# Half-product gate and value projections in three more token blocks of a fused attention and gated feed-forward kernel

## The chip, the cores and the metric

The kernel runs on one core of one Trainium2 chip. The metric is the device time of one execution in microseconds, as the median over several runs. A core has TensorE (PE: matmuls, with weight loads shown as PEld), VectorE (DVE), ScalarE (ACT), GpSimd (POOL) and SyncE (SP), each with its own queue in program order. PSUM, where TensorE writes, has eight banks here, each of 128 partitions by 512 numbers of 32 bits.

## The reference

Inputs are q, k and v of shape (batch 8, heads 8, sequence 576, head size 64), a norm weight of 64 numbers, and four weight matrices. Attention has no softmax; its normalised output is the input x of a gated feed-forward layer:

```
kv  = einsum("bhsd,bhse->bhde", k, v)
o   = einsum("bhsd,bhde->bhse", q, kv)
x   = (o / sqrt(mean(o*o, -1) + 1e-6) * g_norm)   -> 4608 tokens x 512
g   = x @ w_gate        (512 x 1536)
val = x @ w_val         (512 x 1536)
ffn = (gelu(g) * val) @ w_out      (1536 x 512)
out = x + sigmoid(x @ w_res) * ffn
```

## The kernel before

**Tiling.** The 4608 tokens are nine blocks of 512. Blocks 0 to 7 hold the first 512 tokens of each batch; block 8 holds the 64 tokens left over from each of the eight batches, two batches to a slice of 128. Matmul operands are float16, sums are float32 in PSUM.

**A block's stages.** (1) Gate and value: twelve column tiles of 128 columns of each matrix; gelu on ScalarE and the product with the value on VectorE give `hid`. (2) The residual gate: 16 matmuls (`rps`) and tanh. (3) The output phase: `hid @ w_out` and the gate, the sum with x and the store.

**Direct tiles and half products.** A column tile is done directly by `m_gval`: four matmuls of 512 columns for the gate, four for the value. Alternatively `gv_group` does four column tiles at once by splitting tokens, inner dimension and columns in halves and forming seven products in place of eight: 56 matmuls of 256 columns for both matrices, in place of 32 of 512. This needs sums of the weights (`weight_sums`, formed once per group of four tiles, tiles named ws) and sums of the tokens (`token_sums`, once per block, tile ts). `GROUPS` lists which of the three groups of a block go by products: groups 1 and 2 in blocks 2 to 5, all three in blocks 6, 7 and 8; block 1 does none, block 0 one. What is left over is done directly, first. The output phase uses the same scheme with its own sums (`out_by_products`).

**A group's words.** `gv_group` runs a list of words, each a step for gate (g) or value (v):

```
1g 1v Eg 5g Ev 5v dg 6g dv 6v Fg 2g Fv 2v 7g g11 7v cg 3g cv 3v h11 g22 4g g12 h12 4v g21 h22 h21
```

A word with a digit first is a product of four matmuls (L736). Products 1, 6, 7 and 4 go through PSUM bank A, 2 adds to E, 5 and 3 use F. E is a seed, A copied to bank E on ScalarE (L746); d keeps product 5 in SBUF on ScalarE (L750); F and c are VectorE sums of A and d (L757), F back to PSUM and c to SBUF; g is a gelu of a quarter on ScalarE (L767); h the product with the value, on VectorE, or on POOL for quarter 22 (L773). Product 6 overwrites A after E has read it, 7 after F has, 4 after c has. The next group begins in another A bank and swaps E and F.

**Other work is hung between.** The order on each queue is written out by hand. `at(block, slot, ...)` puts functions behind a slot: slots 0 to 11 are the column tiles (a group takes the slot of its first tile), 12 and on are the residual gate and output phase. `at_word(block, i, word, ...)` puts them behind a word of the block's i-th group, `aside_out(block, key, ...)` inside the output phase, whose keys in order are D, gates, F, 00, 22, 01, 11, end. pf (L531) is the gating of a quarter by VectorE, c22 the sum ahead of the last quarter; fin (L535) the sum with x on POOL.

**Attention runs two blocks ahead.** In block m, `plan_attn_ahead` computes batch b = m + 2: `by_token` (L129, two halves on ScalarE) reorders q; `d_qT` and `d_rem_qT` (L363, L371) are transposing DMAs on SP of q and of the 64 left-over rows; `load_behind` makes POOL wait for these (copies into `hold`, L1136 to L1140) and then issues the loads of batch b + 1; `a_rem_kv` forms k-v sums on TensorE and the left-over output (`rem_mm`, L272), `kv_out` and `rem_out` (L281, L291) copy them out; `a_o` (L230) is the output of the 512 tokens; `a_ss` squares on ScalarE (L249) and reduces on VectorE (L254); `a_norm` is the inverse root on POOL, twelve small steps (L306 to L319, result ny); `a_t` (L345) scales by it, `a_x` (L359) by the norm weight; `d_xT` (L376) transposes x by DMA. Part of `a_t`, `a_x` and `d_xT` falls into block m + 1. Until now batch 7 alone, whose scaling falls into block 6, has these at words of groups; batches 4 to 6 have them at slots of direct tiles.

**Buffers.** A tag names a ring of buffers; a new tile waits for the last reader of the one that held its place.

Of the kernel before, what the change touches and what calls it, by code (L numbers as in the profile page):

```python
# [8 lines left out]
FP32 = mybir.dt.float32  # L9
# [9 lines left out]
def kernel(  # L19
# [18 lines left out]
    C = H * D  # L38
# [89 lines left out]
    def by_token(b, copy=nc.vector.tensor_copy, js=slice(0, NJ)):  # L128
        copy(  # L129
            out=b16_t[b, "q"].rearrange("p j h d -> p h j d")[:, :, js, :],  # L130
            in_=raw[b, "q"].rearrange("p h (j d) -> p h j d", j=NJ)[:, :, js, :],
        )
# [35 lines left out]

    def attn_begin(b):
        st[b] = {  # L170
            "qT": attnp.tile([P, NJ, NP, P], FP16, tag="qT", name="qT"),
            "kv2": (
                attnp.tile([P, NP, D], FP16, tag="kv2", bufs=4, name="kv2")
                if b > 0
                else consts.tile([P, NP, P], FP16, name="kv0")
            ),
            "ss": attnp.tile([P, NJ + 1, H], FP32, tag="ss", name="ss"),
            "o": {},
        }
# [101 lines left out]
        nc.scalar.copy(out=st[b]["kv2"], in_=st[b]["ps"][0])  # L281

    def rem_out(b):
        if b < B - 1:
            o32 = attnp.tile([P, C], FP32, tag="o32", name="o32")
        else:
            o32 = qkvp.tile([P, H, NJ * D], FP16, tag="k16", name="o32")
            o32 = o32.rearrange("p a b -> p (a b)").bitcast(FP32)[:, 0:C]
        st[b]["o"][NJ] = o32
        for e in range(2):  # L290
            nc.scalar.copy(  # L291
                out=o32.rearrange("p (r e d) -> p r e d", e=2, d=D)[:, :, e, :], in_=st[b]["ps"][1][e]
            )
# [207 lines left out]
    def out_by_products(blk, later, banks, amid):  # L501
        w = {}
        s_ = hid_sums

        def aside(ahead_of):
            for f in amid.get(ahead_of, ()):
                f()

        def res(jj):
            for j in (2 * jj, 2 * jj + 1):  # L510
                m_res(blk, j, banks[j])

        def first_two():
            for n in ("D", "E", "F", "A"):
                w[n] = pmoe.tile([P, 2, CH], FP32, name="w" + n, bank=banks[n])
            w["d"] = attnp.tile([P, 2, CH], FP32, tag="o32", name="wd")
            s_last(blk)
            prod(w["A"], a_of(blk, 1, 1), b_of(1, 1), True)
            nc.scalar.copy(out=w["E"], in_=w["A"])
            aside("D")  # L520
            prod(w["D"], s_[0], wo_t[:, 0], True)
            nc.scalar.copy(out=w["d"], in_=w["D"])
            aside("gates")
            for j in range(NJ):
                m_sigmoid(j)

        def part(jj):
            return slice(None), slice(2 * jj[0], 2 * jj[0] + 2), slice(jj[1] * CH, (jj[1] + 1) * CH)

        def pf(jj, src):  # L530
            nc.vector.tensor_tensor(out=res_all[part(jj)], in0=th_all[part(jj)], in1=src, op=ALU.mult)  # L531

        def fin(jj):
            of = part(jj)
            nc.gpsimd.tensor_tensor(out=res_all[of], in0=res_all[of], in1=t_t[blk][of], op=ALU.add)  # L535

        def store(jj):
            dst = out[blk * S : blk * S + M0, :].rearrange("(p j) c -> p j c", j=NJ)
            js = slice(2 * jj, 2 * jj + 2)
            nc.sync.dma_start(out=dst[:, js, :], in_=res_all[:, js, :])  # L540

        def others():


            prod(w["A"], s_[1], wo_t[:, 1], False)
            aside("F")
            sub(nc.vector, w["F"], w["A"], w["d"], ALU.add)
            aside("00")
            prod(w["E"], a_of(blk, 1, 2), b_of(2, 1), False)
            pf((0, 0), w["E"])  # L550
            aside("22")
            prod(w["A"], s_[2], wo_t[:, 2], False)
            c22 = res_all[part((1, 1))]
            sub(nc.vector, c22, w["A"], w["d"], ALU.add)
            aside("01")
            prod(w["F"], s_[3], b_of(2, 2), False)
            pf((0, 1), w["F"])
            aside("11")
            prod(w["A"], a_of(blk, 2, 2), wo_t[:, 3], False)
            if len(GROUPS.get(blk + 1, ())) * GF < NF or blk + 1 >= LAST[0]:  # L560
                pf((1, 1), c22)
                pf((1, 0), w["A"])
            else:
                pf((1, 0), w["A"])
                pf((1, 1), c22)
            aside("end")
            if later:
                return
            for i in (1, 0):
                fin((i, i))  # L570
                fin((i, 1 - i))
                store(i)

        if later:
            x = [lambda j=j: a_x(blk, j) for j in range(NJ)]
            at_word(blk + 1, 0, "Fv", x[0])
            at_word(blk + 1, 0, "h21", *x[1:3], lambda: fin((0, 0)), lambda: fin((0, 1)), lambda: store(0))
            at_word(blk + 1, 1, "Fv", x[3], lambda: fin((1, 0)), lambda: fin((1, 1)), lambda: store(1))
        return [lambda: res(0), lambda: res(1), first_two, others]

    def out_last(blk, banks):
# [22 lines left out]
        def run():  # L604
            wa = [bank(1, banks["A"][e]) for e in range(2)]
            wd, we, wf = [bank(2, banks[n]) for n in "DEF"]
            d = attnp.tile([P, 2, CH], FP32, tag="o32", name="wd")
            u = attnp.tile([P, 2, CH], FP32, tag="sq", bufs=3, name="u")
            one = (slice(0, 1), slice(1, 2))
            s_last(blk)  # L610
# [96 lines left out]
    def gv_group(blk, g, banks, amid):  # L707
# [44 lines left out]
        def plus(u, n):  # L752
            if n == "F":
                dst = tile_of("F", u)
            else:
                dst = sb["c", u] = attnp.tile([P, 2, PR], FP32, tag="o32", name="c")
            nc.vector.tensor_tensor(out=dst, in0=ps["A", u], in1=sb["d", u], op=ALU.add)  # L757

        quarter = {"11": ("E", 0, 0), "12": ("F", 0, 1), "21": ("A", 1, 0), "22": ("c", 1, 1)}
# [383 lines left out]
    def at(blk, slot, *fs):  # L1143
        plans[blk].setdefault(slot, []).extend(fs)
# [19 lines left out]
            at(m, 10 + j // 2, lambda j=j: a_x(b, j))  # L1164
        at(m, 11, lambda: d_xT(b, 0, NJ))

    GROUPS = {blk: (1, 2) for blk in range(2, B - 2)} | {B - 2: (0, 1, 2), B - 1: (1, 0, 2), B: (0, 1, 2)}
    amid_gv = {}

    def at_word(blk, i, word, *fs):  # L1170
        amid_gv.setdefault((blk, i), {}).setdefault(word, []).extend(fs)

    def plan_attn_ahead(b):

# [6 lines left out]
            begin.append(lambda: d_rem_qT(b))  # L1181
        if m in GROUPS:
            for i in range(2):
                at(m, 2 + i, lambda i=i: by_token(b, act, slice(2 * i, 2 * i + 2)))
            at(m, 3, *begin)
            if b + 1 < B:
                at(m, 2 * GF, lambda: load_behind(b))
        else:
            at(m, 8, lambda: by_token(b, act, slice(0, 2)))
            at(m, 9, lambda: by_token(b, act, slice(2, 4)), *begin)  # L1190
            at(m, NF - 1, lambda: a_kv(b, act))
            at(m, NF, lambda: load_behind(b))
        if rem:
            own = 2 * pair(b) + 1 == b
            at_word(m, 1, "5v" if own else "3v", lambda: a_rem_kv(b))
            at_word(m, 1, "5v" if own else "g12", lambda: kv_out(b))
            at_word(m, 1, "h21", *[lambda: rem_mm(b)] * own, lambda: rem_out(b), lambda: a_sq(b, NJ))
        at(m, NF, lambda: a_o(b), *[lambda: a_red(b, NJ)] * rem, lambda: a_ss(b, 0), lambda: a_ss(b, 1))
        aside_out(m, "D", lambda: a_ss(b, 2), lambda: a_ss(b, 3))
        aside_out(m, "F", lambda: a_norm(b, 0, NJ + rem, pool))  # L1200
        first = [lambda: new_block(b), lambda: a_t(b, 0), lambda: a_t(b, 1)]
        if b == B - 1:
            aside_out(m, "11", *first)
        else:
            at(m, NF + 3, *first)
        if b == B - 1:
            t = [lambda j=j: a_t(b, j) for j in range(NJ + 1)]
            x = [lambda j=j: a_x(b, j) for j in range(NJ + 1)]
            for i, word, fs in (
                (0, "1v", t[2:3]),  # L1210
                (0, "Fv", t[3:4]),
                (0, "h21", t[4:5]),
                (1, "1v", x[0:2]),
                (1, "Fv", x[2:3]),
                (2, "1v", [x[3], lambda: d_xT(b, 0, NJ), x[4], lambda: d_xT(b, NJ, NJ + 1)]),
            ):
                at_word(m + 1, i, word, *fs)
            return
# [13 lines left out]
    at(0, 6, *sums["v", 2][0:2])  # L1232
    at_word(0, 0, "Fv", *sums["v", 2][2:4])
    late_sums = [f for u in (("g", 0), ("v", 0)) for f in sums[u]]
    for i, f in enumerate(late_sums):
        at_word(2 + i // 2, i % 2, "Fv", f)
    for blk in GROUPS:
        t = token_sums(blk, nc.vector)
        if blk == 2:
            at(blk - 1, NF + 3, *t)  # L1240
            continue
        whole = blk == B - 2 and len(GROUPS[blk]) * GF == NF
        for key, f in zip(("00", "22", "01", "end" if whole else "11"), t):
            aside_out(blk - 1, key, f)
    out_at = {}

# [153 lines left out]
```

## Time and profile before

| | us |
|---|---|
| median of 5 runs | 326.55 (326.1 to 326.95) |
| the profiled execution, its run | 326.95 |
| its span, first to last instruction | 325.1 |
| TensorE busy | 317.0 |
| VectorE busy | 260.4 |
| ScalarE busy | 194.6 |
| POOL busy | 135.5 |

Spans of blocks in that execution, from TensorE's first instruction of each:

| block | start | end of gate and value | end |
|---|---|---|---|
| 2 | 91.80 | 112.09 | 125.40 |
| 3 | 125.40 | 145.64 | 158.94 |
| 4 | 158.94 | 179.18 | 192.48 |
| 5 | 192.48 | 212.97 | 226.28 |
| 6 | 226.28 | 244.96 | 257.58 |
| 7 | 257.58 | 275.92 | 288.55 |

A row of the profile names line, engine, operation and tiles; lengths of matmuls include their passage through the array and so overlap. A group row gives busy time, mean length and the idle time in front of it with what ended that. In a row of stages the columns are bounds, length, busy time and count of PE, PEld, DVE, ACT and POOL, TensorE's granted clock, DMA share and GB/s.

### The profile page before, as it was taken

What the parts mean: (1) busy time and instruction counts of PE and PEld (TensorE: products, weight loads), DVE (VectorE), ACT (ScalarE), POOL (GpSimd) and SP (SyncE); (2) the same over time, 40 slices, a digit from 0 to 9 for tenths busy, and PEclk for the clock granted to TensorE, in tenths of its full rate; (3) what the DMA queues carried; (4) which work ended last, traced back from release to release, by engine and by line L of the source; (5) the groups of instructions that cost most, each with busy time, mean ns of one, the idle gap of its engine ahead of it and who ended that gap; (6) DMA issues with size and microseconds to landing.
All of it is one profiled execution on the core that took longest, in us unless ns stands there. A gap on an engine that the chain in (4) does not pass through costs nothing.

```text
span 325.1 us, 7256 instructions
## 1 busy us (share of the span) xinstructions
PE 317.0 (97%) x2864; PEld 230.0 (71%) x2864; DVE 260.4 (80%) x477; ACT 194.6 (60%) x355; POOL 135.5 (42%) x205
## 2 busy tenths in 40 slices
PE   8989999999999999999999999999999999999993
PEld 3644754444858776787678676868887888788782
DVE  5788879669698999888888888798987677667754
ACT  3673685465727781868267837584766467636660
POOL 2793251572711787037712773114711242043232
PEclk9999999999999999999999999999999999999999
DMA  7999999699995499559958894900331030002004
GB/s 251 325 204 203 195 206 173 162 186 125 157 136 105 150 133 163 156 92 129 100 176 116 102 127 151 145 0 3 129 59 26 0 131 1 2 19 112 3 0 129
DMA packets 76692, 38.87 MB, mean 120 GB/s; under 512 B 42098, under 2 KB 74354, under 8 KB 76658
## 3 DMA queue, kind: packets, MB, share of 16 engines
q0 software_dynamic: 38752, 17.17, 42.0%
q1 hardware_dynamic: 37328, 20.71, 25.3%
q10 hardware_dynamic: 578, 0.52, 0.5%
q8 instruction: 22, 0.36, 0.5%
q14 instruction: 12, 0.10, 0.1%
HBM read 38.80 MB, written 9.44 MB: 148 GB/s over the span
## 4 chain that ended last, share of the span: by engine, by line
PE 96%; DVE 3%; issue 0%; DVEq 0%
PE wA L492 11%; PE Av L736 10%; PE Ag L736 10%; PE rps L419 10%; PE gps L399 9%; PE vps L399 9%; PE Fg L736 5%; PE Fv L736 5%; PE fps L436 3%; PE wF L492 3%; PE wE L492 3%; PE wD L492 3%; PE w L492 2%; PE Ev L736 2%; PE Eg L736 2%; PE idle L901 2%
## 5 line engine op out<-in xcount | busy, mean ns | idle before, releaser
L773 POOL TENSOR_TENSOR hid<-ge,c 128x512 f16<-128x512 f16 x18 | 20.9, 1162 | 84.8 <-ACT ge L767 84.8
L387 ACT ACTIVATE ge<-gps 128x512 f16<-128x512 f32 x36 | 21.3, 597 | 42.3 <-PE gps L399 42.2
L535 POOL TENSOR_TENSOR osb<-osb,t 128x512 f32<-128x512 f32 x28 | 31.8, 1164 | 32.8 <-DVE osb L531 31.0
L492 PEld LDWEIGHTS <-hid_s 128*128 128x128 f16 x384 | 37.6, 98 | 4.3
L399 PE MATMUL gps<-xT,wg 128*128 128x512 f16 x136 | 34.9, 379 | 0.0
L399 PE MATMUL vps<-xT,wv 128*128 128x512 f16 x136 | 34.9, 379 | 0.0
L419 PE MATMUL rps<-wr,xT 128*128 128x512 f16 x144 | 33.4, 380 | 0.0
L388 DVE TENSOR_TENSOR hid<-ge,vps 128x512 f16<-128x512 f16 x36 | 24.5, 685 | 9.3 <-PE vps L399 8.7
L492 PEld LDWEIGHTS <-hid 128*128 128x128 f16 x288 | 28.2, 98 | 5.0
L736 PEld LDWEIGHTS <-wsv 128*128 128x128 f16 x288 | 28.1, 98 | 3.9 <-issue 0.3
L736 PEld LDWEIGHTS <-wsg 128*128 128x128 f16 x288 | 28.1, 98 | 3.4
L757 DVE TENSOR_TENSOR Fg<-Ag,d 128x512 f32<-128x512 f32 x18 | 12.6, 699 | 16.9 <-PE Ag L736 13.4
L428 ACT ACTIVATE th<-rps 128x512 f32<-128x512 f32 x36 | 21.1, 594 | 7.8 <-PE rps L419 7.8
L399 PEld LDWEIGHTS <-wv 128*128 128x128 f16 x136 | 13.3, 98 | 16.1
L254 DVE TENSOR_REDUCE ss<-sq 128x8 f32<-128x512 f32 x32 | 20.1, 679 | 4.4 <-ACT sq L249 4.4
L419 PEld LDWEIGHTS <-xT 128*128 128x128 f16 x144 | 13.5, 98 | 14.2
L399 PEld LDWEIGHTS <-wg 128*128 128x128 f16 x136 | 13.1, 98 | 14.7 <-issue 0.2
L736 PEld LDWEIGHTS <-wg 128*128 128x128 f16 x216 | 20.9, 98 | 3.6
L767 ACT ACTIVATE ge<-c 128x512 f16<-128x512 f32 x18 | 11.3, 630 | 19.8 <-DVE c L757 19.8
L736 PEld LDWEIGHTS <-wv 128*128 128x128 f16 x216 | 21.1, 98 | 2.5
L736 PE MATMUL Av<-ts,wsv 128*128 128x256 f16 x144 | 21.6, 272 | 0.0
L736 PE MATMUL Ag<-ts,wsg 128*128 128x256 f16 x144 | 21.6, 273 | 0.0
(187 smaller groups left out, 741.5 us busy)
## 6 DMA issues: line engine op xcount, KB each, us to landing
out_dram<-osb SPq DMA_DIRECT2D x14, 512.0 KB, 2.7
qraw<-in_q_dram POOLq DMA_DIRECT2D x7, 512.0 KB, 6.8
k<-in_k_dram POOLq DMA_DIRECT2D x7, 512.0 KB, 8.5
v<-in_v_dram POOLq DMA_DIRECT2D x7, 512.0 KB, 10.9
wg<-in_moe_w_gate_dram POOLq DMA_DIRECT2D x2, 512.0 KB, 8.2
wv<-in_moe_w_val_dram POOLq DMA_DIRECT2D x2, 512.0 KB, 8.6
wo<-in_moe_w_out_dram POOLq DMA_DIRECT2D x2, 512.0 KB, 14.0
out_dram<-osb SPq DMA_DIRECT2D x4, 256.0 KB, 4.5
```

Of the source, the lines that this page charges most:

```text
L254: nc.vector.tensor_reduce(out=out_, in_=sqs.pop((b, i)), op=ALU.add, axis=mybir.AxisListType.X)
L387: nc.scalar.activation(out=ge, in_=gps, func=AF.Gelu)
L388: nc.vector.tensor_tensor(out=hids[blk][:, f, :], in0=ge, in1=vps, op=ALU.mult)
L399: nc.tensor.matmul(ps[:, j0 * P : j1 * P], lhsT=w[:, cc, :], rhs=xT_t[blk][:, j0:j1, cc, :], start=(cc == 0 and j0 == 0), stop=(cc == NP - ...
L419: nc.tensor.matmul(rps, lhsT=xT_t[blk][:, j, cc, :], rhs=wr16[:, cc, :], start=(cc == 0), stop=(cc == NP - 1),)
L428: nc.scalar.activation(out=th, in_=rps, func=AF.Tanh, scale=0.5)
L492: nc.tensor.matmul(ps[:, e - es[0], :], lhsT=a[:, f, e * P : (e + 1) * P], rhs=b[:, f, :], start=(start and e == es[0] and f == 0), stop=( ...
L535: nc.gpsimd.tensor_tensor(out=res_all[of], in0=res_all[of], in1=t_t[blk][of], op=ALU.add)
L736: nc.tensor.matmul(out_[:, r, :], lhsT=lhsT, rhs=rhs, start=(first and r == 0 and c == 0), stop=(c == 1), skip_group_check=True,)
L757: nc.vector.tensor_tensor(out=dst, in0=ps["A", u], in1=sb["d", u], op=ALU.add)
L767: nc.scalar.activation(out=ge[q], in_=source(q, "g"), func=AF.Gelu)
L773: eng.tensor_tensor(out=dst, in0=ge[q], in1=source(q, "v"), op=ALU.mult)
```

## The change

Blocks 3, 4 and 5 get all three groups by half products (`WHOLE = 3`); block 2 stays as it was, and blocks 6 to 8 too. What stood at slots of direct tiles moves: the copies of q to word g11 of groups 0 and 1, with the begin of attention and its transposes behind the second; the k-v sums and the left-over rows to the last group; the scaling and transposes of batches 4 to 6 to the places that batch 7 had. The last token sum goes ahead of pf(1,1). The weight sums of group 0, which were spread over the groups of blocks 2 to 5, go to slots 2, 6 and 7 and the output phase of block 1. Buffers: one for qT in place of two, three for the tag o32 (c and the left-over output, now for batch 7 too), and wd in the ring of the squares.

```diff
-            "qT": attnp.tile([P, NJ, NP, P], FP16, tag="qT", name="qT"),
+            "qT": attnp.tile([P, NJ, NP, P], FP16, tag="qT", bufs=1, name="qT"),
@@ rem_out
-        if b < B - 1:
-            o32 = attnp.tile([P, C], FP32, tag="o32", name="o32")
-        else:
-            o32 = qkvp.tile([P, H, NJ * D], FP16, tag="k16", name="o32")
-            o32 = o32.rearrange("p a b -> p (a b)").bitcast(FP32)[:, 0:C]
+        o32 = attnp.tile([P, C], FP32, tag="o32", bufs=3, name="o32")
@@ out_by_products (and out_last alike)
-            w["d"] = attnp.tile([P, 2, CH], FP32, tag="o32", name="wd")
+            w["d"] = attnp.tile([P, 2, CH], FP32, tag="sq", bufs=3, name="wd")
@@ others
-            if len(GROUPS.get(blk + 1, ())) * GF < NF or blk + 1 >= LAST[0]:
+            if whole(blk + 1):
+                pf((1, 0), w["A"])
+                aside("end")
+                pf((1, 1), c22)
+            else:
                 pf((1, 1), c22)
                 pf((1, 0), w["A"])
-            else:
-                pf((1, 0), w["A"])
-                pf((1, 1), c22)
-            aside("end")
@@ gv_group, plus
-                dst = sb["c", u] = attnp.tile([P, 2, PR], FP32, tag="o32", name="c")
+                dst = sb["c", u] = attnp.tile([P, 2, PR], FP32, tag="o32", bufs=3, name="c")
@@
-    GROUPS = {blk: (1, 2) for blk in range(2, B - 2)} | {B - 2: (0, 1, 2), B - 1: (1, 0, 2), B: (0, 1, 2)}
+    WHOLE = 3
+    GROUPS = {blk: (1, 2) for blk in range(2, WHOLE)} | {blk: (0, 1, 2) for blk in range(WHOLE, B - 1)} | {B - 1: (1, 0, 2), B: (0, 1, 2)}
+    def whole(blk):
+        return WHOLE <= blk < B - 1
@@ plan_attn_ahead
             for i in range(2):
-                at(m, 2 + i, lambda i=i: by_token(b, act, slice(2 * i, 2 * i + 2)))
-            at(m, 3, *begin)
+                half = lambda i=i: by_token(b, act, slice(2 * i, 2 * i + 2))
+                if whole(m):
+                    at_word(m, i, "g11", half)
+                else:
+                    at(m, 2 + i, half)
+            if whole(m):
+                at_word(m, 1, "g11", *begin)
+            else:
+                at(m, 3, *begin)
...
+            last = len(GROUPS[m]) - 1
...
-            at_word(m, 1, "5v" if own else "3v", lambda: a_rem_kv(b))
-            at_word(m, 1, "5v" if own else "g12", lambda: kv_out(b))
-            at_word(m, 1, "h21", *[lambda: rem_mm(b)] * own, lambda: rem_out(b), lambda: a_sq(b, NJ))
+            at_word(m, last, "5v" if own else "3v", lambda: a_rem_kv(b))
+            at_word(m, last, "5v" if own else "g12", lambda: kv_out(b))
+            at_word(m, last, "h21", *[lambda: rem_mm(b)] * own, lambda: rem_out(b), lambda: a_sq(b, NJ))
...
-        if b == B - 1:
+        if whole(m + 1):
             aside_out(m, "11", *first)
         else:
             at(m, NF + 3, *first)
-        if b == B - 1:
+        if whole(m + 1):
             t = [lambda j=j: a_t(b, j) for j in range(NJ + 1)]
@@ weight and token sums
-    for i, f in enumerate(late_sums):
-        at_word(2 + i // 2, i % 2, "Fv", f)
+    for i, f in enumerate(late_sums[0:6]):
+        at(1, (2, 6, 7)[i // 2], f)
+    for key, f in zip(("00", "22"), late_sums[6:8]):
+        aside_out(1, key, f)
...
-        whole = blk == B - 2 and len(GROUPS[blk]) * GF == NF
-        for key, f in zip(("00", "22", "01", "end" if whole else "11"), t):
+        for key, f in zip(("00", "22", "01", "end" if whole(blk) else "11"), t):
             aside_out(blk - 1, key, f)
```

More of the change, by code (lines that the diff above doesn't have):

```diff
@@ L606, in run @@
             wd, we, wf = [bank(2, banks[n]) for n in "DEF"]
-            d = attnp.tile([P, 2, CH], FP32, tag="o32", name="wd")
+            d = attnp.tile([P, 2, CH], FP32, tag="sq", bufs=3, name="wd")
             u = attnp.tile([P, 2, CH], FP32, tag="sq", bufs=3, name="u")
```

## The prediction

> **What bounds the kernel now.** I read the shares of busy time and the chain that ended last first, then the busy time by stage, then TensorE's instructions in order of time, and last the engines around one stall. The page's busy shares and its chain by engine:
>
> ```profile
> PE 317.0 (97%) x2864; PEld 230.0 (71%) x2864; DVE 260.4 (80%) x477; ACT 194.6 (60%) x355; POOL 135.5 (42%) x205
> ...
> PE 96%; DVE 3%; issue 0%; DVEq 0%
> ```
>
> TensorE sets the end: 96% of the chain is its own work. A busy TensorE says little by itself, so the next question is whether instructions start back to back. TensorE in order of time, block 5 (start, length, operation); the fourth row opens group 1, the last one group 2:
>
> ```profile
> 192.48 1.03 PE L399 MATMUL gps<-xT,wg 128*128 128x512 f16 x4
> 193.34 1.03 PE L399 MATMUL vps<-xT,wv 128*128 128x512 f16 x4
> ...
> 199.39 0.60 PE L736 MATMUL Ag<-xT,wg 128*128 128x256 f16 x4
> ...
> 205.50 0.60 PE L736 MATMUL Ag<-xT,wg 128*128 128x256 f16 x4
> ```
>
> The lengths overlap, so starts count. Four direct columns of gate and value take 199.39 - 192.48 = 6.91 us (32 matmuls of 512 columns), the same four columns by half products 205.50 - 199.39 = 6.11 us (56 of 256 columns). No idle time stands in either. The exchange is worth **0.80 us** wherever it is fed.
>
> Busy time by stage (bounds, length, then PE, PEld, DVE, ACT, POOL with counts, clock, DMA): the gate and value stages of blocks 3, 4 and 5 as they are, then of blocks 6 and 7, which already do all three groups by products:
>
> ```profile
> 125.40:145.64 20.24, 20.24 (x203) 14.93 (x201) 17.91 (x34) 12.81 (x23) 7.25 (x7) 1.00 0.70 131
> 158.94:179.18 20.24, 20.24 (x203) 14.94 (x200) 17.92 (x34) 12.81 (x23) 7.26 (x7) 1.00 0.59 118
> 192.48:212.97 20.49, 20.49 (x202) 14.80 (x200) 17.02 (x33) 12.94 (x23) 6.43 (x6) 1.00 0.56 119
> 226.28:244.96 18.68, 18.68 (x171) 16.41 (x168) 17.59 (x33) 12.43 (x24) 7.38 (x7) 1.00 0.32 92
> 257.58:275.92 18.34, 18.34 (x170) 16.43 (x168) 13.28 (x22) 12.35 (x24) 7.31 (x7) 1.00 0.15 59
> ```
>
> Block 7 is three groups at 6.11 us with nothing lost. Block 6 is 0.34 us longer: it also carries the scaling of batch 7 on VectorE (17.59 us busy of 18.68). That is what blocks 3 to 5 are about to look like. Where block 6 loses it: VectorE in order of time, then TensorE's pieces of the chain at that place:
>
> ```profile
> 225.79 1.29 DVE L345 TENSOR_TENSOR t<-op,ny 128x512 f16<-128x512 f32 x2
> 227.00 0.68 DVE L531 TENSOR_TENSOR osb<-th,wA 128x512 f32<-128x512 f32 x1
> ...
> 228.53 0.69 DVE L345 TENSOR_TENSOR t<-op,ny 128x512 f16<-128x512 f32 x1
> 229.13 0.69 DVE L757 TENSOR_TENSOR Fg<-Ag,d 128x512 f32<-128x512 f32 x1
> 229.73 0.69 DVE L757 TENSOR_TENSOR Fv<-Av,d 128x512 f32<-128x512 f32 x1
> ```
>
> ```profile
> 229.94 0.53 PE Ag L736 x4
> 230.47 0.00 issue
> 230.47 0.60 PE Av L736 x4
> ```
>
> A product takes 0.44 us; these two took 0.53 and 0.60. Product 7 overwrites A, so it waits until VectorE's Fg and Fv have read A, and those stand behind a full VectorE queue left from the output phase. Two later products lose 0.04 each: 0.09 + 0.16 + 0.08 = 0.33 us.
>
> **The change, part by part.**
>
> Group 0 by products in blocks 3 to 5. TensorE: -0.80 us in each, **-2.40** in all, if fed. VectorE: two Fg/Fv and two c sums (about 0.69 each) and three hidden products (0.68) for four of 0.68: +2.1 us of durations a block; less the two weight sums that leave each block (four half operations of 0.285, 1.1 us). ScalarE +2.4 us (two seeds, two keeps at 0.6), POOL +1.16 us. The stage then has the VectorE work of block 6, in the same words and order, since batches 4, 5 and 6 now get the placement that batch 7 has. So I take block 6's stall, 0.34 us a block: **+1.02**. Bounds: 0 (block 7's row) and 0.8 (where the gain is eaten).
>
> One rule speaks against this. The Trainium skill, "VectorE: DVE Perf Modes", section "The DRAIN you can't avoid", says that a VectorE operation does not start before the pipe of the one ahead has emptied (it allows an earlier start elsewhere on the page). Read so, the lengths add up. The rows above show starts 0.60 us apart (228.53, 229.13, 229.73) against lengths of 0.69. By the rule, some 14 operations until VectorE has caught up would end 14 x 0.09 = 1.3 us later, and a block would lose 1.3 + 0.34 - 0.80 = 0.84 us instead of gaining: 329.1 us in all. The measured starts contain whatever drain there is; I go by them.
>
> Scaling of the first two parts (t) ahead of pf(1,0), not after the block. In blocks 2 to 4 this now stands in the output phase, as in block 5 above (225.79 before 227.00). A late norm holds everything queued behind on VectorE: pf(1,0), which frees bank A for ScalarE's seed of Ev, the keeps d behind that seed, and Fg. The norm chain on POOL ends 225.76 - 226.28 = -0.52 us against the end of block 5's output phase; for blocks 2, 3 and 4 the same row ends at 124.88, 158.42 and 191.96, each -0.52 against 125.40, 158.94 and 192.48. So the position is the same, with no slack and no wait: counted in the 0.34.
>
> Query copies (by_token) moved from the direct columns to word g11 of groups 0 and 1: 1.04 us on ScalarE each. In block 6 ScalarE idles 1.50 and 1.03 us just there, waiting for c. Cost 0; if c came early, up to 0.1 us.
>
> Transposing DMAs: d_qT and d_rem_qT on SP now follow the second copy. With block 6's times that copy ends 11.26 us into the block. Two issues of block 4 now, and the landing of all four of the second kind:
>
> ```profile
> 169.59 2.55 SPq L363 DMA_TRANSPOSE qT<-q x1
> 172.31 1.52 SPq L371 DMA_TRANSPOSE qrT<-qr x1
> ...
> DMA to landing us min/median/max: 2.6/3.4/4.4
> ```
>
> The second issue comes at 11.3 + 2.7 = 14.0 and lands at 17.4 (16.6 to 18.4). TensorE wants it after word 3v of the last group: group 2 starts at 238.85 in block 6, twelve words at 0.437 later is 17.8 us into the block. The slack is 0.4 us, with an end of -0.6 in blocks 3 and 4 (batch 7 uses it only at h21). Behind it stand that batch's 40 k-v matmuls and products 4. I take 0: the 4.4 was measured with an xT transpose right in front in the queue, which now comes after. That xT pair ends near 19 us on SP and lands by about 22; the token sums read it at 28. POOL's hold ahead of the next loads comes after the last group, some 19 us, behind both landings. Half 0 of the copy, 1.1 us earlier than before, needs q: loads land 6.2 to 6.8 us after issue there, 8 us and more ahead of the copy.
>
> Token sum 4 ahead of pf(1,1), and pf order as block 5 has it: no operation added, cost 0.
>
> Weight sums of group 0 in block 1: eight of about 0.5 us. Slots 2, 6 and 7 hold two each (1 us); VectorE idled 1.46, 0.98 and 1.04 us at those slots, and the two left go to gaps of 0.60 and 0.57 us. POOL runs the norm beside some: one such pair took 0.88 instead of 0.48 beside a POOL operation. Then slots 6 and 7 run 0.8 us over, within the two-slot turn (3.46 us) of the banks. Cost 0; without that cover 0.5.
>
> Buffers: one qT less (its reader a_o ended a block ago), wd in the squares' turn (its predecessor was reduced over 2 us earlier: reductions end at 183.9, wd is written at 186.31), a third o32. Cost 0 each; a wait would show on ScalarE's wd copy.
>
> **Sum.** Blocks 3 and 4 hold 20.24 - 6.91 - 2 x 6.11 = 1.11 us of k-v matmuls and their gaps: 18.68 + 1.11 = 19.79, -0.45 each. Block 5: 1.36 likewise, 20.04 against 20.49, -0.45. Together **-1.35**. The profiled execution took 326.95 (span 325.1 and 1.85 around it), so its like would take 325.6, span 323.75. It lies 0.40 above the median of the runs; on the median, 326.55 - 1.35 = **325.2 us**.
>
> **The rivals.** *No stalls at all:* the end-of-stage slack absorbs them and TensorE gets 2.40 plus 0.1 of today's: 324.05. For it: block 7; against it: block 6 with the same VectorE queue. *Late remainder transpose:* qrT lands at its worst in blocks 3 and 4 and the wait is 0.6 each: 325.2 + 1.2 = 326.4, no change to speak of. *Slower:* the norm. Moved ahead of pf(1,0), each us that POOL's chain is late stalls product 7 in group 0 one for one, in blocks 3, 4 and 5, where before only the scaling itself slipped. From 0.45 us a block the gain is gone, from 0.7 us it is a loss that counts; at 0.9 us: 326.55 + 3 x 0.45 = 327.9. For it: zero slack, and loads' descriptors on POOL ahead of the chain in blocks 2 to 4 (not in block 5); against it: the chain began when its sums were ready and ended at the same -0.52. *That the products don't pay* is excluded by 6.11 against 6.91.
>
> **How the numbers follow.** About 0.2%, 0.65 us, is what a measurement of this kernel can tell from no change. Likeliest case 0.62 (324.6 to 325.8), no stalls 0.13, late transpose 0.12, late norm 0.10, other mixtures 0.03. The first two are faster: 0.75, and a little of the third: 0.77; the rest of the third and mixtures within: 0.12; slower 0.11. The range runs from 324.0 to 326.4: it takes in the first three cases and leaves 0.13 outside.
>
> **What would show it.** Right: stages of blocks 3 to 5 near 19.8, 19.8 and 20.0 us, short waits only at product 7 of group 0, copies of q in ScalarE's idle time ahead of c, qrT landed before 3v. Wrong: stages near 19.4 (no stalls), TensorE waiting at kvp L272 for qrT, VectorE's t waiting for POOL's ny, or block 1 longer than now.

## The result, and the profile after

The changed kernel takes 325.41 us as a median (325.19 to 326.15, 23 runs) beside 326.41 us for the kernel before (44 runs): a ratio of 0.9969, 95% interval 0.9962 to 0.9976, so about 1.0 us or 0.3% faster. The forecast was 325.2 us, or -1.35.

The profiled execution spans 324.0 us against 325.1. The busy shares and the chain by engine, after:

```profile
PE 316.0 (98%) x2936; PEld 236.8 (73%) x2936; DVE 265.6 (82%) x486; ACT 200.8 (62%) x367; POOL 140.0 (43%) x208
...
PE 96%; DVE 3%; issue 0%; DVEq 0%
```

TensorE still sets the end. The gate and value stages of blocks 2 to 6, after (columns as before):

```profile
91.56:111.80 20.24, 20.24 (x203) 14.93 (x201) 18.65 (x36) 12.81 (x23) 6.44 (x6) 1.00 0.71 115
125.10:145.01 19.91, 19.91 (x226) 17.24 (x224) 18.82 (x34) 14.83 (x27) 8.37 (x8) 1.00 0.65 129
158.31:178.23 19.92, 19.92 (x226) 17.21 (x224) 18.83 (x34) 14.82 (x27) 8.38 (x8) 1.00 0.49 121
191.53:211.71 20.18, 20.18 (x226) 17.15 (x224) 18.23 (x33) 15.16 (x27) 7.78 (x7) 1.00 0.51 113
225.02:243.83 18.81, 18.81 (x171) 16.41 (x168) 17.72 (x33) 12.43 (x24) 7.28 (x7) 1.00 0.36 84
```

Against 20.29, 20.24, 20.24, 20.49 and 18.68 before, blocks 2 to 6 change by -0.05, -0.33, -0.32, -0.31 and **+0.13** us, -0.88 together. The other 0.25 us of the span lies ahead of block 1, which begins at 55.14 in place of 55.39; over the profiles of this study, with the same opening, block 1 begins anywhere from 54.51 to 55.39, so that part is not the change's. The stages are read from one profiled execution of each kernel; a stage that no edit touches repeats closely (block 7 takes 18.34 us in all twelve profiles), so differences of 0.1 us in a stage count.

Blocks 3 to 5 gain less than the 0.45 us forecast, and block 6, whose gate and value stage is not among those changed, loses. Where, in TensorE's pieces of the chain in block 3 (start, length, group; L732 is L736 of the kernel before), with the undisturbed pieces of 0.44 left out:

```profile
128.76 0.54 PE Ag L732 x4
129.29 0.00 issue
129.29 0.60 PE Av L732 x4
...
131.20 0.47 PE Av L732 x4
...
135.61 0.60 PE Av L732 x4
```

The first three waits are those of block 6 before (0.53, 0.60 and 0.48 there). The last is product 7v of group 1, 0.16 us late. In block 6 before, the same product lost only 0.04:

```profile
236.78 0.48 PE Av L736 x4
```

The longer wait of 0.60 stands in blocks 4, 5 and 6 too.

### The profile page after: what moved, and what is told of

Same layout as the page of the kernel before. It is cut to its first block, busy times and chain, and to the rows that moved or that the text cites. A ratio compares the mean times of both kernels' runs of the same rounds, so it can differ in the third digit from the quotient of the medians.

```text
span 324.0 us, 7446 instructions
## 1 busy us (share of the span) xinstructions
PE 316.0 (98%) x2936; PEld 236.8 (73%) x2936; DVE 265.6 (82%) x486; ACT 200.8 (62%) x367; POOL 140.0 (43%) x208
## 4 chain that ended last, share of the span: by engine, by line
PE 96%; DVE 3%; issue 0%; DVEq 0%
PE Av L732 12%; PE Ag L732 12%; PE wA L488 11%; PE rps L415 10%; PE gps L395 6%; PE vps L395 6%; PE Fv L732 6%; PE Fg L732 6%; PE fps L432 3%; PE Eg L732 3%; PE wF L488 3%; PE wE L488 3%; PE Ev L732 3%; PE wD L488 3%; PE w L488 2%; PE idle L897 2%
## 5 line engine op out<-in xcount | busy, mean ns | idle before, releaser
L732 PEld LDWEIGHTS <-wsv 128*128 128x128 f16 x336 | 32.7, 98 | 5.6 <-issue 1.6
L732 PEld LDWEIGHTS <-wsg 128*128 128x128 f16 x336 | 32.7, 98 | 4.3
L742 ACT COPY Eg<-Ag 128x512 f32<-128x512 f32 x21 | 12.0, 571 | 28.6 <-PE Ag L732 28.3
L383 ACT ACTIVATE ge<-gps 128x512 f16<-128x512 f32 x24 | 14.1, 597 | 21.3 <-PE gps L395 21.2
L732 PEld LDWEIGHTS <-wv 128*128 128x128 f16 x252 | 24.6, 98 | 3.0
L732 PEld LDWEIGHTS <-wg 128*128 128x128 f16 x252 | 24.4, 98 | 3.3
L732 PE MATMUL Av<-ts,wsv 128*128 128x256 f16 x168 | 25.2, 272 | 0.0
L732 PE MATMUL Ag<-ts,wsg 128*128 128x256 f16 x168 | 25.2, 272 | 0.0
L395 PE MATMUL gps<-xT,wg 128*128 128x512 f16 x88 | 22.6, 379 | 0.0
L395 PE MATMUL vps<-xT,wv 128*128 128x512 f16 x88 | 22.6, 379 | 0.0
L488 PE MATMUL wA<-wo_ts,hid_s 128*128 128x256 f16 x168 | 20.6, 273 | 0.0
L384 DVE TENSOR_TENSOR hid<-ge,vps 128x512 f16<-128x512 f16 x24 | 16.3, 686 | 4.8 <-PE vps L395 4.0
```

What stands on the lines that cost most here:

```text
L383: nc.scalar.activation(out=ge, in_=gps, func=AF.Gelu)
L384: nc.vector.tensor_tensor(out=hids[blk][:, f, :], in0=ge, in1=vps, op=ALU.mult)
L395: nc.tensor.matmul(ps[:, j0 * P : j1 * P], lhsT=w[:, cc, :], rhs=xT_t[blk][:, j0:j1, cc, :], start=(cc == 0 and j0 == 0), stop=(cc == NP - ...
L488: nc.tensor.matmul(ps[:, e - es[0], :], lhsT=a[:, f, e * P : (e + 1) * P], rhs=b[:, f, :], start=(start and e == es[0] and f == 0), stop=( ...
L732: nc.tensor.matmul(out_[:, r, :], lhsT=lhsT, rhs=rhs, start=(first and r == 0 and c == 0), stop=(c == 1), skip_group_check=True,)
```

## The experiments

All are compared with the kernel before on the same chip. The stage of a block is from its first gate matmul to its first residual-gate matmul. One correction to the expectations below: 20.09 for block 5 was read with too early a bound; its length is 20.18, and with 0.12 less 20.06.

### What makes the new wait

`ts_behind` puts the last token sum back behind pf(1,1):

```diff
             if whole(blk + 1):
                 pf((1, 0), w["A"])
-                aside("end")
                 pf((1, 1), c22)
+                aside("end")
```

> The changed kernel with the last token sum put back behind pf(1,1), nothing else. The changed kernel loses a second time in each of blocks 3 to 6, at product 7v of group 1 (0.60 us in place of 0.44), which block 6 did not do before the change. Theory[...]: the token sum ahead of pf(1,1) starts POOL's four sums (fin) 0.33 us later, so POOL's product h22 (1.16 us) now overlaps VectorE's scaling of the left-over rows (t<-o, both inputs in SBUF), which took 0.81 in place of 0.68 and holds the Fg and Fv behind it. Then this kernel has t<-o at 0.68, stages of blocks 3, 4, 5 and 6 near 19.79, 19.80, 19.97 and 18.68 us (0.12 less each), 0.5 us less in all: ratio to the kernel before 0.9954. Rival, VectorE is simply full and any order is as late: stages stay at 19.91, 19.92, 20.09 and 18.80, ratio 0.9969.

Measured: 324.98 us, ratio 0.9962 (0.9949 to 0.9974). Its stages of blocks 3 to 6:

```profile
124.52:144.31 19.79, 19.79 (x227) 17.26 (x224) 18.70 (x34) 14.83 (x27) 8.50 (x8) 1.00 0.63 128
157.61:177.40 19.79, 19.79 (x227) 17.25 (x224) 18.70 (x34) 14.82 (x27) 8.50 (x8) 1.00 0.50 122
190.70:210.74 20.04, 20.04 (x226) 17.12 (x224) 18.09 (x33) 15.15 (x27) 7.88 (x7) 1.00 0.54 115
224.05:242.73 18.68, 18.68 (x171) 16.43 (x168) 17.59 (x33) 12.43 (x24) 7.40 (x7) 1.00 0.36 87
```

They are 0.12, 0.13, 0.14 and 0.13 us shorter, 0.52 together, and block 6 is back at 18.68. The total's interval overlaps that of the changed kernel (0.9962 to 0.9976), so the totals alone don't tell the two apart; the stages do.

`no_fin` keeps VectorE's order and takes away what POOL was late for. It leaves out the sum with x on POOL for blocks 2 to 5:

```diff
             for i in (1, 0):
-                fin((i, i))
-                fin((i, 1 - i))
+                if not whole(blk + 1):
+                    fin((i, i))
+                    fin((i, 1 - i))
                 store(i)
```

> The changed kernel without POOL's sum with x in blocks 2 to 5 (what is stored there lacks the x term); VectorE's and ScalarE's order is untouched, the last token sum still stands ahead of pf(1,1). Theory[...]: with no fin ahead of it POOL's h22 of group 0 starts as soon as its gelu is done, some 0.8 us earlier, and is over before t<-o begins; t<-o takes 0.68, product 7v of group 1 does not wait, stages of blocks 3 to 6 are 0.12 us shorter each (19.79, 19.80, 19.97, 18.68). Rival, the order on VectorE alone makes the second wait: t<-o may be shorter, but the stages stay at 19.91, 19.92, 20.09, 18.80. The wait at product 7 of group 0 (0.09 and 0.16 us) stays under both[...].

Measured: stages of 19.79, 19.79, 20.04 and 18.67 us, ratio 0.9966 (0.9951 to 0.9981). The gain of `ts_behind` in the stages, with VectorE's order untouched. The scaling of the left-over rows on VectorE beside POOL's product h22, first the changed kernel in block 3, VectorE then POOL:

```profile
132.87 0.81 DVE L341 TENSOR_TENSOR t<-o,ny 128x512 f16<-128x512 f32 x1
```

```profile
131.97 1.16 POOL L769 TENSOR_TENSOR hid<-ge,c 128x512 f16<-128x512 f16 x1
```

and the kernel without the sums:

```profile
132.40 0.68 DVE L341 TENSOR_TENSOR t<-o,ny 128x512 f16<-128x512 f32 x1
```

```profile
130.75 1.16 POOL L770 TENSOR_TENSOR hid<-ge,c 128x512 f16<-128x512 f16 x1 [6.65 <-ACT ge L764]
```

In the first pair POOL works until 133.13 and the VectorE operation beside it is 0.13 us longer; in the second POOL ends at 131.91, half a microsecond earlier than VectorE begins. That the one waits for the other shows in the ends: VectorE's row ends 0.55 us behind POOL's, 133.68 against 133.13, and does so in all four blocks. In block 4 it is 166.90 against 166.35:

```profile
166.08 0.82 DVE L341 TENSOR_TENSOR t<-o,ny 128x512 f16<-128x512 f32 x1
```

```profile
165.19 1.16 POOL L769 TENSOR_TENSOR hid<-ge,c 128x512 f16<-128x512 f16 x1
```

So the token sum put ahead of pf(1,1) cost through POOL: it delayed pf(1,1), with it the four sums of 1.1 us each, then h22, and h22 then met the one VectorE operation behind which the next Fg and Fv stood. The margin is thin: in `ts_behind` h22 ends at 132.34, 0.05 us after VectorE's scaling has begun, and the scaling takes its 0.68 us.

### What the rest of the change costs, and whether blocks add

`whole6` and `whole5` set `WHOLE = 6` and `WHOLE = 5`, nothing else.

> The changed kernel with groups as before: blocks 3 to 5 do group 0 directly, so only the rest of the change is in (weight sums of group 0 in block 1, last token sum ahead of pf(1,1) before block 6, one qT, o32 and squares' rings). Theory: the rest costs nothing but the 0.12 us in block 6; the weight sums that left blocks 2 to 5 give at most 0.05 us back. Stage of block 1 as long as before (36.4 us to the end of its output phase), stages of blocks 3, 4, 5 at 20.24, 20.24, 20.3 to 20.5, block 6 at 18.80: ratio 1.0000 to 1.0004. Rival: some of the gain comes from the moved weight sums or the buffers and not from the products: ratio 0.998 or less. Rival on the other side: the moved sums cost and hide a part of the gain: ratio over 1.001.

Measured: 1.0005 (0.9996 to 1.0014); stages 20.24, 20.24, 20.49 and 18.82 us, block 1 to the end of its output phase 36.42 (36.41 before). The moved weight sums, 3.4 us more on VectorE in block 1 (30.98 busy in place of 27.57, in the changed kernel), lengthen nothing, and the buffers are free; what remains is the 0.14 us in block 6. The steps that blocks 3 to 5 moved from slots to words are not in this kernel; that they cost nothing there is read from `ts_behind`, whose stages leave no room for it.

> The changed kernel with blocks 3 and 4 done as before, block 5 alone added. Theory, the blocks are independent: stage of block 3 and 4 at 20.24, block 5 at 20.18, block 6 at 18.81; a third of the change's gain, ratio 0.9995. Rival, a later block pays for the earlier ones' backlog: block 5 alone would be shorter than 20.1.

Measured: 0.9995 (0.9981 to 1.0008); stages 20.24, 20.24, 20.17 and 18.81 us. Block 5 alone gives 0.32 us, where it gave 0.31 in the full change: it neither owes anything to blocks 3 and 4 nor pays for them.

### The two rivals that ended badly, priced

`late_norm`, on the changed kernel:

```diff
-        eng.tensor_scalar(out=m, in0=ss, scalar1=1.0 / D, ...)
+        for _ in range(4 if eng is nc.gpsimd else 1):
+            eng.tensor_scalar(out=m, in0=ss, scalar1=1.0 / D, ...)
```

> The changed kernel with the first step of POOL's norm done four times in place of once (same numbers), which makes ny some 0.9 us later (3 x 0.3). It prices the predicted rival. If a late norm holds pf(1,0), the seed of Ev and Fg one for one, VectorE's t waits 0.9 us for ny at the end of the output phase of blocks 2 to 5, and the stages of blocks 3, 4, 5, 6 come to about 20.8, 20.8, 21.0 and 19.7: 3.6 us more than the changed kernel, slower than the kernel before (ratio 1.008). If there is slack in the chain, the stages grow by less than 0.5 us each and the ratio stays under 1.003.

Measured: 1.0084 (1.0054 to 1.0114); stages 20.58, 20.59, 20.84 and 19.46 us, 0.67, 0.67, 0.66 and 0.65 more. VectorE at the end of block 2's output phase, and TensorE's first matmul of block 2:

```profile
125.87 1.29 DVE L342 TENSOR_TENSOR t<-op,ny 128x512 f16<-128x512 f32 x2 [0.59 <-POOL ny L316]
```

```profile
92.15 1.04 PE L396 MATMUL gps<-xT,wg 128*128 128x512 f16 x4 [1.01 <-DMA xT<-t]
```

The scaling begins 0.17 us behind the block's end (125.70) where it began 0.48 ahead in the changed kernel: 0.65 later, and each stage 0.65 to 0.67 longer. One for one, as the rival said, though the delay itself came out smaller than the 0.9 expected. Another 1.0 us of this execution is TensorE's wait for block 2's x, shown in the row of L396. The delay had a part in that too: this x goes through the same norm, its transpose was issued 25.13 us into block 1 in place of 24.72, and it then took 12.4 us to land in place of 10.3 (see the last section).

`late_q` puts the second copy of q and the transposes behind it at g21:

```diff
-                    at_word(m, i, "g11", half)
+                    at_word(m, i, ("g11", "g21")[i], half)
...
-                at_word(m, 1, "g11", *begin)
+                at_word(m, 1, "g21", *begin)
```

> The changed kernel with the second half of the q copy, and the transposes behind it, at word g21 of group 1 in place of g11: ScalarE ends the copy some 2.7 us later. It prices the other rival. In the changed kernel the left-over rows' transpose landed 1.7 us (block 3) and 1.8 us (block 4) ahead of the matmuls that read it. So TensorE should wait 0.9 to 1.1 us ahead of kvp L272 in blocks 3 and 4 and not in block 5, where it is read later: stages 20.9, 20.9, 20.1; ratio 1.003. If the landing takes less when it comes later, or something else sets that place, the wait is under 0.5 us.

Measured: 1.0068 (1.0045 to 1.0091); stages 21.66, 20.86 and 20.18 us. TensorE in block 3:

```profile
144.80 0.22 PE L272 MATMUL kvp<-kv,qrT 64*64 64x64 f16 x2 [1.42 <-DMA qrT<-qr]
```

It waited 1.42 us in block 3 and 0.6 in block 4 (2.0 in both), not in block 5. The place and the blocks are those expected, and so is the sum of the waits; the split was not, nor the total, 1.0068 for 1.003. Of the 1.75 and 0.94 us by which the stages grew, 0.33 us each are not in that wait. Most of it lies ahead of the wait: the second copy now runs before ScalarE's seed Eg of group 2, which starts 13.91 us into block 3 in place of 13.38, and TensorE is 0.26 us (block 4: 0.24) behind when it comes to qrT.

### Where the gain can be had

`spread`, with the last token sum as in `ts_behind` and:

```diff
-                (0, "1v", t[2:3]),
-                (0, "Fv", t[3:4]),
+                (0, "Fv", t[2:3]),
+                (0, "cv", t[3:4]),
                 (0, "h21", t[4:5]),
-                (1, "1v", x[0:2]),
-                (1, "Fv", x[2:3]),
-                (2, "1v", [x[3], lambda: d_xT(b, 0, NJ), x[4], lambda: d_xT(b, NJ, NJ + 1)]),
+                (1, "Fv", x[0:1]),
+                (2, "1v", [*x[1:4], lambda: d_xT(b, 0, NJ)]),
+                (2, "Fv", [x[4], lambda: d_xT(b, NJ, NJ + 1)]),
```

> The changed kernel with the last token sum behind pf(1,1) and VectorE's scaling placed later: t2 and t3 behind Fv and cv of group 0 in place of 1v and Fv, x0 behind Fv of group 1, x1 to x3 behind 1v of group 2 and x4 behind its Fv, in place of 1v and Fv of group 1. The same operations, none removed. Theory, the waits at product 7 are a VectorE backlog of some 8 operations that clears within the stage: Fg and Fv of group 0 come 0.3 us earlier, groups 0 and 1 lose at most 0.05 us each, and the idle 0.9 us of group 2 takes the rest. Stages of blocks 3, 4, 5, 6 near 19.5, 19.5, 19.7 and 18.4 us, 1.6 us less than the changed kernel in all: ratio to the kernel before 0.992. Rival, the stage is bound by VectorE's total: the wait moves to products of group 1 or 2 and the stages shrink by no more than the 0.12 us of the token sum, ratio 0.9954.

Measured: **323.76 us**, ratio 0.9926 (0.9914 to 0.9938), the fastest of all kernels here. Its stages of blocks 3 to 6:

```profile
124.56:144.10 19.54, 19.54 (x226) 17.25 (x224) 18.89 (x34) 14.90 (x27) 8.51 (x8) 1.00 0.65 131
157.40:176.90 19.50, 19.50 (x227) 17.25 (x224) 18.87 (x34) 14.91 (x27) 8.50 (x8) 1.00 0.50 123
190.20:209.95 19.75, 19.75 (x226) 17.18 (x224) 18.03 (x33) 15.10 (x27) 7.76 (x7) 1.00 0.55 116
223.26:241.65 18.39, 18.39 (x171) 16.44 (x168) 17.76 (x33) 12.51 (x24) 7.40 (x7) 1.00 0.30 88
```

VectorE is as busy as before (18.89 us in block 3, 18.82 in the changed kernel), so its total was not the bound: 19.44 us (three groups at 6.11 and 1.11 of k-v matmuls) is all but reached. `spread_t` makes only the first half of the move (t2 and t3; the weightings x stay where the changed kernel has them).

> The first half of spread alone: the last token sum behind pf(1,1) and t2, t3 behind Fv and cv of group 0; x0 to x4 stay behind 1v and Fv of group 1 and 1v of group 2. Theory, the waits are a VectorE backlog: moving t2 and t3 frees Fg and Fv of group 0, so group 0 loses under 0.1 us, but VectorE has the same work to the end of group 1 and TensorE now arrives there 0.25 us earlier, so products 7 and 7v of group 1 wait 0.3 to 0.45 us. Stages of blocks 3 and 4 stay between 19.7 and 19.85 us, block 6 at 18.6 to 18.75: as ts_behind, ratio 0.996. Rival, each wait has its own cause and group 0's was the order of t2 and t3: stages 19.5, as spread, ratio 0.993.

Measured: 0.9991 (0.9977 to 1.0006); stages 20.00, 19.99, 20.25 and 18.89 us, so 0.2 us more than `ts_behind` and not the same. VectorE and then TensorE in its block 3:

```profile
127.25 0.70 DVE L753 TENSOR_TENSOR Fg<-Ag,d 128x512 f32<-128x512 f32 x1 [0.26 <-ACT d L746]
...
133.91 0.69 DVE L753 TENSOR_TENSOR Fg<-Ag,d 128x512 f32<-128x512 f32 x1
134.51 0.69 DVE L753 TENSOR_TENSOR Fv<-Av,d 128x512 f32<-128x512 f32 x1
```

```profile
134.65 0.60 PE Ag L732 x4
135.25 0.00 issue
135.25 0.60 PE Av L732 x4
```

Group 0's Fg came early enough, but VectorE now idled 0.26 us ahead of it, which t2 had filled, and had the same queue to clear up to group 1's Fg. Group 1's Fg begins 9.26 us into the block where it began at 9.04 in `ts_behind` (133.56): 0.22 us later, and the stage is 0.21 longer. A backlog moves with its work: only moving the weightings on into group 2 removed it. `spread` has the same 0.26 us of idle time ahead of group 0's Fg and loses nothing by it.

### Block 2 as well: two attempts

`whole2_spread` is `spread` with `WHOLE = 2`, batch 3 without left-over rows, and block 2's token sums in block 1's output phase.

> The kernel spread (scaling placed later, last token sum behind pf(1,1)) with block 2 done by products too, its token sums in the output phase of block 1. Theory: a fourth exchange of 0.80 us is fed like the others; block 2 has block 1's four weightings more on VectorE and batch 3's left-over rows less. Stage of block 2 near 19.6 in place of 20.24 us, 0.6 us less in all: ratio to the kernel before 0.9907. Rival: the extra weightings of block 1's x in group 0 bring the wait back, stage 20.0, ratio 0.992.

Measured: 1.0063 (1.0035 to 1.0090), runs from 326.67 to 331.97; stage of block 2 22.65 us. TensorE waited 1.8 us for qrT, since block 1's second store stood ahead of the transpose of q on SP and waited for POOL's sums. `whole2_order` puts block 1's weightings and sums behind the transposes and block 2's four token sums to the places "11" and "end" of block 1's output phase:

```diff
-            at_word(blk + 1, 0, "Fv", x[0])
-            at_word(blk + 1, 0, "h21", *x[1:3], ...)
-            at_word(blk + 1, 1, "Fv", x[3], ...)
+            at_word(blk + 1, 0, "h21", x[0])
+            at_word(blk + 1, 1, "cv", *x[1:3], ...)
+            at_word(blk + 1, 1, "h21", x[3], ...)
```

> whole2_spread lost 2.4 us in block 2: block 1's second store stood ahead of the transpose of q on SP and waited for POOL's sums, so the left-over rows' transpose landed 1.8 us late; and the token sums of block 2 waited for its x to land from the transposing DMA. Here block 1's weightings, sums and stores stand behind the transposes (words cv and h21 of group 1), and the token sums of block 2 behind 11 and end. Theory: the wait at kvp L272 is gone and block 2's stage is 19.6 to 19.9 us; if block 2's x lands by the end of block 1 (90.5 us where it was seen last) the ratio is 0.991. Rival: the landing of x is what spoils it, TensorE waits for it at the start of block 2 by 0.5 us and more, and the ratio is 0.993 or above with a wide spread of runs.

Measured: 1.0081 (1.0059 to 1.0103); stage of block 2 25.33 us. Neither expectation held. The wait for qrT is gone, and x landed in time, but now VectorE and TensorE show:

```profile
105.69 4.59 DVE L355 TENSOR_TENSOR t<-t,g 128x512 f16<-128x512 f16 x4
110.20 0.69 DVE L753 TENSOR_TENSOR Fg<-Ag,d 128x512 f32<-128x512 f32 x1
```

```profile
110.94 1.01 PE L732 MATMUL Ag<-ts,wsg 128*128 128x256 f16 x4 [3.28 <-DVE Fg L753]
111.75 1.06 PE L732 MATMUL Av<-ts,wsv 128*128 128x256 f16 x4
```

Four weightings took 4.59 us, where two take 0.75 in the runs above. The last three one by one, and the POOL operation beside each:

```profile
106.32 1.38 DVE L355 TENSOR_TENSOR t<-t,g 128x512 f16<-128x512 f16 x1
107.62 1.37 DVE L355 TENSOR_TENSOR t<-t,g 128x512 f16<-128x512 f16 x1
108.91 1.37 DVE L355 TENSOR_TENSOR t<-t,g 128x512 f16<-128x512 f16 x1
```

```profile
106.07 1.34 POOL L769 TENSOR_TENSOR hid<-ge,c 128x512 f16<-128x512 f16 x1
107.38 1.33 POOL L531 TENSOR_TENSOR osb<-osb,t 128x512 f32<-128x512 f32 x1
108.67 1.33 POOL L531 TENSOR_TENSOR osb<-osb,t 128x512 f32<-128x512 f32 x1
```

Each weighting ends 0.28 or 0.29 us behind the end of its POOL operation. A good order for block 2 is left open.

## Why the prediction was right

It held in direction and range and was 0.35 us too good on the gain (1.35 forecast, 1.0 measured). That the time itself came nearer, 325.41 us for 325.2, is luck: the median of the kernel before fell from 326.55 to 326.41 with more runs. Of the signs named for being right, "short waits only at product 7 of group 0" did not come.

**The exchange, -0.80 us a block:** right. With nearly all waits removed in `spread` the stage of block 3 is 19.54 us, 0.70 below 20.24; the new group 0 takes 6.16 us there and group 1 6.11, and the 0.10 us that the stage keeps above 19.44 is short waits (0.01, 0.04 and 0.05).

**Block 6's stall, +0.34 a block:** right for the waits it named: product 7 of group 0 shows 0.54 and 0.60 in the new blocks, as 0.53 and 0.60 in block 6 before. `ts_behind`, with 19.79, 19.79 and 20.04 us, gives the very stages of the sum. That the starts of VectorE operations count and not their lengths held too: in block 3 they stand at 127.35, 127.95 and 128.55, and the blocks gain 0.31 to 0.33 us where the rule with added lengths would have them lose 0.84.

**"Token sum 4 ahead of pf(1,1), and pf order as block 5 has it: no operation added, cost 0":** this step failed. It cost 0.12 to 0.14 us in each of four blocks, 0.5 us in all and in block 6 too, which the sum had not touched at all. The step looked at VectorE, where the two operations only change places, and not at who waits for pf(1,1): POOL, whose queue the prediction never followed from there to h22. The scaling beside h22 takes 0.81 us in place of 0.68 and ends 0.55 us behind it. The Trainium skill, "SBUF — State Buffer", section "Who interferes with whom", says that a VectorE instruction with two SBUF inputs contends with a GpSimd instruction that reads SBUF, for a port that one of them holds alone; the rows agree. The prediction used such a delay for the weight sums and did not ask which other operation it could meet.

**The moved norm and transposes at no cost:** right, with different margins. The norm has no slack (0.65 us late cost 0.65 to 0.67 in each stage). The left-over rows' transpose landed 1.8 us ahead in block 3 (issue at 138.49, 2.8 us to landing, read at 143.1), not 0.4: it was issued 13.4 us into the block and not 14.0, and took 2.8 us and not 3.4. The prediction put the longer landings down to an xT in front in the queue; in `late_q`, with none in front, block 3's took 3.6 us, so that cause stays open.

**Weight sums, buffers:** right. `whole6` shows no cost of either, and `ts_behind`, where the buffers are in full use, leaves no room for one.

The measured median gains a little more than the stages' 0.88 us; the interval of the ratio, 0.8 to 1.2 us, contains it.

## What to carry to other kernels

When two operations change places on one engine at no cost, follow whoever waits for the one that moved back, through its own queue to what it runs beside; here 0.5 us of a forecast 1.35 went that way. A stall behind a full queue is a backlog: taking work from ahead of the stalled operation helps only if that work goes past the next deadline as well. And a queue position without slack is worth pricing, by making the thing late, before more is put on it.

## What the runs showed of the hardware that was not expected

VectorE operations with both inputs in SBUF, interleaved with POOL operations that read SBUF, can each wait for a POOL operation: four that take about 0.4 us each took 4.59 in `whole2_order`, and two took 1.62 in `whole2_spread`. VectorE operations with one input in PSUM keep their 0.68 us beside the same POOL operations (`hid` from Av at 105.09 in `whole2_order`, with POOL at work from 104.96 to 106.11). The 3.28 us in which TensorE then stood idle also cost it clock:

```profile
98.00:107.00 9.00, 9.00 (x85) 8.07 (x83) 8.73 (x17) 7.84 (x14) 4.00 (x4) 1.00 0.39 47
110.90:114.40 3.50, 3.46 (x16) 2.22 (x15) 2.56 (x4) 1.23 (x2) 0.72 (x1) 0.51 1.06 260
```

The granted clock is 1.00 in the first stretch, ahead of the pause, and 0.51 in the second, right behind it; the products there start 0.81 to 0.85 us apart in place of 0.44. The Trainium skill ("TensorE: Matmul & The Clock Gate", section "What's actually happening") describes a clock gate that goes to half rate after an idle window of about 3.4 us. The row's 3.28 us counts from the modelled end of the last product; from 0.44 us behind that product's start, 107.06, to 110.94 it is 3.44 us by that estimate, which fits the page. A stall of that length costs more than itself: here some 1.6 us more, by an estimate from four products of 0.41 us extra each.

The transpose of block 2's x takes 10.4 us to land in the kernel before, where all ten transposes of x have a median of 4.4. POOL issues the loads of a later batch at the same time, and the landing goes with the order of the two: in the five profiles here in which the transpose is issued ahead of the first load it lands in 8.0 to 9.5 us, in the seven in which it follows in 9.7 to 12.4. The 12.4 is `late_norm`, where it follows by 0.53 us; in the other six it is 0.16 at most. No run changes this order alone, so the cause is argued and not shown.
